# Attention and two feed-forward layers in one kernel: pooled V in one overlapping read, V without zero rows, a split first score, copies moved to VectorE, and a new written order

## The chip, the cores and the metric

The kernel runs on one core of a Trainium2 chip. The core has five engines that take their instructions in order and meet through semaphores: TensorE (PE, with its weight loads PEld), VectorE (DVE), ScalarE (ACT), GpSimd (POOL), and SyncE (SP), which here issues DMAs. The metric is the device time of one execution in microseconds (us). Before the change three runs took 609.0, 609.87 and 610.14 us; the median is 609.87 us.

## The reference, cut to what matters

Two batches of eight heads attend over 768 positions of head size 64. Each query sees the keys nearer than 16 positions, and in the same softmax 24 pooled keys (the maximum over blocks of 32) with pooled values (the mean over blocks of 32). The result, 1536 tokens of 512 features, goes through two feed-forward layers, 512 to 2048 to 512, with different activations.

```
k_sum = k.reshape(B, H, nb, 32, D).max(axis=3)
v_sum = v.reshape(B, H, nb, 32, D).mean(axis=3)
scores_l = where(|pos_q - pos_k| < 16, q @ k.T / sqrt(D), -1e9)
scores_s = q @ k_sum.T / sqrt(D) + log(32)
a = softmax(concat([scores_l, scores_s]))
x = a @ concat([v, v_sum])
r = relu(x @ w_in);  x = (s * r * r + b) @ w_out          # first layer
h = x @ w_in2;       out = max(0.01 * h, h) @ w_out2      # second layer
```

## The kernel before, in words

**Attention in units.** A unit is one of 6 groups of 256 queries with one of 4 pairs of heads, so there are 24 units; units 0 to 7 make the first 512 tokens. Within a unit four windows of 64 queries see 96 near keys each and 24 pooled ones, so a score row has 120 columns. The written codes of a unit's steps are: `s` scores on PE (L207), `x` masked score and its minimum on DVE (L230), `e` exponential on ACT (L246), `r` reciprocal on DVE (L258, L259), `n` normalisation on POOL (L268), `t` transposition on PE (L279), `c` copy out of PSUM on ACT (L287), `o` product with V on PE (L296), `y` and `Y` the high part on ACT (L307) and the low part on DVE (L312) of the result `xt`. The pooled keys are made by `km` on DVE (L121) and put between the near keys by `kp` on POOL (L132, L136). The pooled values come from `p` on PE (L173), `wc` copies them to SBUF (L179), `w` stores them to DRAM in 4 DMAs (L185), and `vs` reads them back to rows 96 to 119 of each V tile, one DMA per window (L195).

**Feed-forward in steps.** Every product is made of three fp32r matmuls (high by high, low by high, high by low). A step is one of 16 slices of 128 hidden features for one chunk of 512 tokens: `I` (L366, two halves of 6 matmuls), `A` and `a` (activation on ACT and on DVE, L377 and L384), `G` and `g` (high part on ACT, L391, low part on DVE, L398), and `O` (L415, four parts of 3 matmuls). There are 96 steps; the first 16 are chunk 0 of the first layer. During these 16 the weights of the first layer come in as 64-bit words of 512 KB per half step: `L` loads one into one of four stage tiles (L320), `R` rescales its upper half on ACT (L326), `B` puts the 32-bit value together on DVE in two instructions (L336, L337) and by that frees the stage tile for a later load. `H` and `lp` or `lv` split a weight tile for use: high part on ACT (L351), low part on POOL (`lp`) or on DVE (`lv`), both at L357.

**What sets the order.** No scheduler moves anything: the string `HEAD` is read from left to right, and each engine, and SP's queue, gets its instructions in that order. The number behind a code is the unit, the half step or the part. From step 33 on a plain loop writes the rest. A wait at the head of one engine's queue therefore holds up all that is written behind it on that engine. All DMAs but three constants and one store are issued by SP.

Of the kernel before, what the change touches and what calls it, by code (L numbers as in the profile page):

```python
# [48 lines left out]
k0 mask q0 iden k1 pool q2 km0 kp0 q1 k2 s0 v1 v0 km1 v2 s1 x0 kp1 L0 e0 k3 s2 x1 q3 e1 s3 r0 vn1 km2 n0 x2 kp2 t0  # L49
e2 r1 s4 x3 n1 q4 c0 r2 s5 x4 e3 n2 t1 t2 q5 c1 x5 e4 r3 n3 c2 r4 p0 n4 e5 t3 p1 c3 r5 p2 n5 R0 km3 t4 wc0 B0 kp3 c4  # L50
t5 w0 s6 c5 H0 L2 s7 x6 lp0 e6 s8 x7 vs0 s9 e7 r6 x8 n6 vs1 x9 t6 e8 r7 n7 o0 vs2 c6 r8 y0 n8 t7 e9 Y0 vn0 o1 vn2 L1
t8 k4 o2 y1 r9 c7 L3 Y1 n9 L4 o3 y2 c8 Y2 t9 y3 o4 c9 Y3 o5 y4 Y4 p3 y5 Y5 o6 R1 o7 R2 B1 y6 o8 y7 Y6 L6 H1 p4 Y7 y8
B2 lp1 R3 I0 wc1 Y8 L8 km4 v3 H2 o9 R4 lp2 B3 I1 y9 B4 kp4 H3 L5 I2 A0 lp3 Y9 L9 H4 s10 a0 v4 lp4 G0 I3 x10 q6 e10
g0 I4 A1 r10 O2 n10 R5 a1 I5 R6 B5 G1 t10 B6 L7 A2 O1 c10 O0 g1 L10 H6 O3 a2 lp6 O5 H5 s11 G2 lp5 R7 g2 I6 R8 x11
e11 O9 B7 I7 B8 R9 L11 O7 R10 r11 O4 L12 A3 B10 n11 O11 H8 O8 a3 H10 L13 lp8 t11 B9 O6 R11 lp10 I8 c11 B11 L14 H7 w1
O10 R12 lp7 I9 G3 B12 L17 R13 g3 L15 I10 H9 k7 B13 R14 lp9 O13 A4 B14 L16 O15 H12 O12 lp12 a4 L23 I11 k5 G4 R15 I12
g4 A5 B15 H14 O17 lp14 a5 O19 L18 R16 O16 km7 R17 I13 B16 kp7 I14 A6 B17 L20 H16 O14 km5 L19 lp16 R18 I15 a6 H11 kp5
B18 G5 O18 s12 H13 g5 L21 G6 I16 lv11 H18 lv13 R19 lp18 O21 g6 R20 O23 B19 A7 O25 R21 O27 B20 L22 q7 O20 x12 O22 L28
# [12 lines left out]
O85 G22 r21 I47 g22 H47 lv47 I48 H50 A23 lp50 t18 a23 I49 c18 G23 o18 A24 g23 H52 t19 n21 a24 I50 y18 c19 Y18 lp52
t20 t21 c20 I51 c21 I52 H54 A25 lp54 o19 a25 I53 y19 Y19 I54 H56 lp56 s22 s23 x22 e22 I55 x23 e23 r22 O91 O90 O95
H58 r23 O94 lp58 O89 O88 O93 G24 O92 H49 g24 o20 H51 lv49 o21 A26 n23 lv51 G25 O99 a26 n22 y21 O97 y20 g25 I56 Y20
A27 Y21 O103 a27 I57 O101 H60 O96 lp60 O98 O100 G26 O102 H53 g26 I58 H55 lp53 A28 t22 G27 a28 lp55 t23 I59 c22 g27
c23 I60 A29 H62 a29 O106 lp62 I61 O107 H64 O105 lp64 O111 O109 O104 O110 H57 O108 G28 lv57 I62 H59 g28 G29 lv59 O115
A30 g29 O112 o22 a30 o23 y22 Y22 O116 y23 Y23 O119 O114 I63 O118 H66 O113 A31 lp66 I64 a31 G30 H61 g30 O117 lv61 I65
H63 G31 lp63 O123 H68 g31 O120 A32 lp68 O121 a32 O122 O125 H65 O126 X5 lv65 O124 G32 Z5 I66 X4 g32 X6 Z4 O127 X7 Z7
O131 Z6 O130 O128 I67 A33 H67 a33 lp67 G33 g33 O129
'''
POOL_BIAS = math.log(BLK)  # L80


@with_exitstack
def block_attention_moe_moe(ctx, tc, q, k, v, vn, w1, w2, mask, ident_in, pool_in, out):
# [13 lines left out]
    soft = pool("soft", 4)  # L98
# [3 lines left out]
    ps_at = pool("ps_at", 2, space=PSUM)  # L102
# [94 lines left out]
    def att_scores(n, ps, tag):  # L197
        g, hp = n
        b, gb = divmod(g, GPB)
        sc = ps.tile([P, 512], F32, name=tag)  # L200
# [13 lines left out]
        scs[n] = sc  # L214

    def att_max(n, ring=None):
# [3 lines left out]
        if ring is None:  # L220
            sm = soft.tile([P, 512], F32, name="sm")[:, : GU * KEYS].rearrange("p (u c) -> p u c", u=GU)
# [6 lines left out]
        for u in range(GU):  # L228
# [10 lines left out]
            )  # L239
        sms[n] = sm, nm  # L240
# [207 lines left out]
    def place(kind, n):  # L448
# [16 lines left out]
        "s": lambda n: att_scores(units[n], *place("s", n)),  # L465
        "x": lambda n: att_max(units[n], wres if n < 8 else None),
# [81 lines left out]
def _layout(q, k, v, moe_w_in, moe_w_out, moe_s, moe_b, moe2_w_in, moe2_w_out):  # L548
# [8 lines left out]
    vp = np.zeros((NG, P, GU, DM), f32)  # L557
    vp[:, :LOC] = vw.reshape(NG, GU, LOC, DM).transpose(0, 2, 1, 3)
# [53 lines left out]
```

## Time and profile before

| what | value |
|---|---|
| median of three runs | 609.87 us |
| span of the profiled execution, first to last instruction | 606.2 us, 3.7 us under that median |
| PE busy | 586.1 us, 97% |
| DVE, ACT, POOL busy | 360.6, 333.1, 196.7 us |
| moved by DMA | 54.33 MB |

The page has no time of the profiled execution other than its span; the 3.7 us stand for what lies around it. Busy times say little on their own here, since the span has two very different parts: the first 126 us or so, in which attention, the conversion of the weights and the first 16 steps share all engines, and the rest, in which PE goes from matmul to matmul.

### The profile page before, as it was taken

How to read it: one execution, taken by the hardware profiler on the slowest of the kernel's cores; microseconds unless marked ns; L12 is line 12 of the kernel's file. 1: busy time of each engine (PE TensorE's matmuls, PEld its weight loads, DVE VectorE, ACT ScalarE, POOL GpSimd, SP SyncE). 2: the span in 40 equal slices, each digit the busy share in tenths (PEclk: the TensorE clock that was granted, in tenths of full speed). 3: DMA queues.
4: the chain of work that ended last, by engine and by line, in shares of the span. 5: the costliest groups of instructions: out<-in, count | busy, mean ns of one | idle time of the engine just before them, and what ended most of it. 6: DMA issues, size and time to landing. Idle time of an engine off the chain costs nothing.

```text
span 606.2 us, 8728 instructions
## 1 busy us (share of the span) xinstructions
PE 586.1 (97%) x3208; PEld 475.0 (78%) x3208; DVE 360.6 (59%) x689; ACT 333.1 (55%) x709; POOL 196.7 (32%) x182
## 2 busy tenths in 40 slices
PE   5799899999999999999999999999999999999997
PEld 4467687777878888888888888888888888888885
DVE  4668997872636334567777867766544444544443
ACT  4978577654648554555555655554544444544442
POOL 2644546354235343223322233222222222222220
PEclk9999999999999999999999999999999999999999
DMA  8897876400024000004342433310100000100001
GB/s 334 288 315 276 271 250 211 165 1 2 1 104 170 2 2 1 0 5 135 104 115 96 139 105 95 118 66 1 70 0 2 0 1 0 71 0 1 0 1 69
DMA packets 17058, 54.33 MB, mean 90 GB/s; under 512 B 2152, under 2 KB 2792, under 8 KB 16376
## 3 DMA queue, kind: packets, MB, share of 16 engines
q1 hardware_dynamic: 16440, 53.29, 26.1%
q10 hardware_dynamic: 576, 0.50, 0.3%
q8 instruction: 25, 0.41, 0.3%
q14 instruction: 17, 0.14, 0.1%
HBM read 50.21 MB, written 3.57 MB: 89 GB/s over the span
## 4 chain that ended last, share of the span: by engine, by line
PE 80%; DVE 9%; DMA 4%; ACT 3%; SPq 1%; issue 1%; POOL 1%; DVEq 0%; POOLq 0%; ACTq 0%
PE h L366 37%; PE acc L417 22%; PE acc L415 18%; DVE w L337 3%; DMA st<-in_w 2%; DVE w L336 2%; DMA kt<-in_k 2%; PE at L207 1%; PE at L296 1%; DVE g L398 1%; ACT st L326 1%; PE at L279 1%; SPq L195 1%; DVE r L384 1%; DVE kp L121 1%
## 5 line engine op out<-in xcount | busy, mean ns | idle before, releaser
L366 PE MATMUL h<-xt,win 128*128 128x512 f32 x1152 | 283.2, 392 | 2.8 <-DVE r L384 2.0
L366 PEld LDWEIGHTS h<-xt,win 128*128 128x128 f32 x1152 | 214.5, 188 | 50.9 <-issue 2.3
L357 POOL TENSOR_TENSOR win<-w,win 128x512 fp32r<-128x512 f32 x96 | 133.3, 1389 | 311.9 <-ACT win L351 308.4
L415 PE MATMUL acc<-g,wout 128*128 128x512 f32 x576 | 144.6, 393 | 1.7 <-DVE g L398 1.7
L417 PE MATMUL acc<-wout,g 128*128 128x512 f32 x576 | 138.2, 389 | 0.0
L415 PEld LDWEIGHTS acc<-g,wout 128*128 128x128 f32 x576 | 106.8, 188 | 25.4 <-DVE g L398 2.5
L417 PEld LDWEIGHTS acc<-wout,g 128*128 128x128 f32 x576 | 108.1, 188 | 22.5
L357 DVE TENSOR_TENSOR wout<-w,wout 128x512 fp32r<-128x512 f32 x78 | 86.6, 1112 | 39.0 <-ACT wout L351 38.8
L379 ACT ACTIVATE r<-h 128x512 f32<-128x512 f32 x48 | 28.7, 597 | 87.5 <-PE h L366 87.5
L386 DVE TENSOR_TENSOR r<-r,h 128x512 f32<-128x512 f32 x48 | 33.0, 688 | 68.6 <-ACT r L379 68.4
L351 ACT CAST wout<-w 128x512 fp32r<-128x512 f32 x96 | 59.5, 620 | 24.1 <-PE acc L415 11.7
L351 ACT CAST win<-w 128x512 fp32r<-128x512 f32 x96 | 59.1, 616 | 19.4 <-PE h L366 15.4
L384 DVE SCALAR_TENSOR_TENSOR r<-r,msk,h 128x512 f32<-128x512 f32 x48 | 35.7, 744 | 33.5 <-ACT r L377 33.2
L337 DVE SCALAR_TENSOR_TENSOR w<-st,w 128x512 int32<-128x512 int32 x64 | 52.4, 819 | 4.8 <-ACT st L326 0.7
L398 DVE SCALAR_TENSOR_TENSOR g<-r,msk,g 128x512 fp32r<-128x512 f32 x48 | 41.2, 858 | 23.7 <-ACT g L391 23.6
L393 ACT CAST g<-r 128x512 fp32r<-128x512 f32 x48 | 29.8, 621 | 36.4 <-DVE r L386 36.4
L391 ACT ACTIVATE g<-r,msk 128x512 fp32r<-128x512 f32 x48 | 34.7, 722 | 23.4 <-DVE r L384 16.1
L326 ACT ACTIVATE st<-st 128x512 f32<-128x512 f32 x64 | 41.7, 673 | 9.9 <-DMA st<-in_w 9.9
L402 DVE TENSOR_TENSOR g<-r,g 128x512 fp32r<-128x512 f32 x48 | 33.1, 690 | 22.6 <-ACT g L393 22.6
L377 ACT ACTIVATE r<-h 128x512 f32<-128x512 f32 x48 | 28.4, 591 | 32.3 <-PE h L366 28.8
L357 POOL TENSOR_TENSOR wout<-w,wout 128x512 fp32r<-128x512 f32 x18 | 25.2, 1401 | 33.9 <-ACT wout L351 33.7
L336 DVE TENSOR_SCALAR w<-st 128x512 int32<-128x512 int32 x64 | 32.4, 506 | 1.7 <-DMA st<-in_w 1.7
(50 smaller groups left out, 307.7 us busy)
## 6 DMA issues: line engine op xcount, KB each, us to landing
st<-in_w SPq DMA_DIRECT2D x64, 512.0 KB
vt<-in_v SPq DMA_DIRECT2D x5, 1024.0 KB
kt<-in_k SPq DMA_DIRECT2D x8, 500.0 KB
out<-kt SPq DMA_DIRECT2D x11, 256.0 KB
q<-in_q SPq DMA_DIRECT2D x8, 256.0 KB
w<-in_vn SPq DMA_DIRECT2D x3, 512.0 KB
w<-in_q SPq DMA_DIRECT2D x4, 256.0 KB
w<-in_v SPq DMA_DIRECT2D x2, 512.0 KB
```

Of the source, the lines that this page charges most:

```text
L326: nc.scalar.activation(out=high, in_=high, func=AF.Prelu, scale=2.0**-112, alpha=2.0**32)
L336: nc.vector.tensor_scalar(f, low, 29, None, op0=ALU.logical_shift_right)
L337: nc.vector.scalar_tensor_tensor(out=f, in0=high, scalar=3, in1=f, op0=ALU.logical_shift_left, op1=ALU.bitwise_or)
L351: nc.scalar.copy(t[:, 0, :], wf[layer, fc][:, half, :])
L357: engine.tensor_sub(t[:, 1, :], wf[layer, fc][:, half, :], t[:, 0, :])
L366: nc.tensor.matmul(hs[i], lhsT=w[:, a, cc * P : (cc + 1) * P], rhs=xt[c][:, b, cc, :], start=(cc == 0 and a == b == 0), stop=(cc == NCC - ...
L384: nc.vector.scalar_tensor_tensor(out=r, in0=r, scalar=sb_sb[:, 0:1], in1=h, op0=ALU.mult, op1=ALU.mult)
L391: nc.scalar.activation(out=gs[i][:, 0, :], in_=rs[i], func=AF.Identity, bias=sb_sb[:, 1:2], scale=1.0)
L398: nc.vector.scalar_tensor_tensor(out=g[:, 1, :], in0=r, scalar=sb_sb[:, 1:2], in1=g[:, 0, :], op0=ALU.add, op1=ALU.subtract)
L402: nc.vector.tensor_sub(g[:, 1, :], r, g[:, 0, :])
L415: nc.tensor.matmul(acc[m], lhsT=w[:, a, ms], rhs=g[:, b, :], start=first, stop=last)
L417: nc.tensor.matmul(acc[m], lhsT=g[:, b, ms], rhs=w[:, a, :], start=first, stop=last)
```

## The change

1. `vs` reads all windows of a tile in one DMA, with an access pattern whose windows overlap in DRAM (24 rows, a stride of 16 rows from window to window): 7 DMAs in place of 24.
2. V lies in DRAM with 96 rows per window in place of 128 of which 32 were zero: 768 KB per group in place of 1024 KB.
3. The three constants (`mask`, `pool`, `iden`) are issued by SP, behind the first keys and queries, not by ACT beside them.
4. The scores of unit 0 are made in two sets of matmuls (`sl`: the 96 near columns, `sp`: the 24 pooled ones).
5. Some copies go from ACT or POOL to DVE: `cv` (for `c`), `yv` (for `y`), `kpv` (for `kp`).
6. The attention tiles `sm` and `at` are named buffers handed out by a small class, so their reuse follows the written order.
7. `HEAD` is written anew; among other things more of the low parts of weights are `lv`, on DVE, and fewer are `lp`.

```
-k0 mask q0 iden k1 pool q2 km0 kp0 q1 k2 s0 v1 v0 km1 v2 s1 x0 kp1 L0 e0 k3 s2 x1 q3 e1 s3 r0 vn1 km2 n0 x2 kp2 t0
+k0 km0 q0 iden kp0 k1 q1 s1 mask km1 x1 e1 pool kp1 sl0 sp0 x0 s3 k2 r1 v0 e0 km2 q2 r0 n1 kp2 s2 x2 t1 e2 x3 r2 cv1
...
+class Slots:
+    def tile(self, key):
+        self.used[key] = i = self.idle.pop(0)
+        return self.pool.tile([P, 512], F32, name=f"{self.name}{i}")
+    def free(self, key):
+        if key in self.used:
+            self.idle.append(self.used.pop(key))
...
-            nc.sync.dma_start(t, v[g][:, us, :])
+            nc.sync.dma_start(t[:LOC], v[g][:, us, :])
...
-            of = vps[b][16 * r0 : 16 * (r0 + n) + 8]
-            for u in range(n):
-                nc.sync.dma_start(t[LOC:KEYS, u, :], of[16 * u : 16 * u + 24])
+            of = vps[b]
+            rows = bass.AP(of.tensor, of.offset + 16 * r0 * DM, [[DM, 24], [16 * DM, n], [1, DM]])
+            nc.sync.dma_start(t[LOC:KEYS], rows)
...
-                    sc[hs, u * KEYS : (u + 1) * KEYS],
+                    sc[hs, u * KEYS : (u + 1) * KEYS].rearrange("p (c j) -> p c j", c=WCH)[:, :, lo:hi],
...
-                    rhs=kt[hs, c0 : c0 + WCH, :],
+                    rhs=kt[hs, c0 : c0 + WCH, lo:hi],
...
-        "mask": lambda: nc.scalar.dma_start(msk_sb, mask),
+        "mask": lambda: nc.sync.dma_start(msk_sb, mask),
...
+        "kpv": lambda x: place_k(x // NHP, x % NHP, nc.vector.tensor_copy),
+        "sl": lambda n: att_scores(units[n], *place("s", n), 0, CH),
+        "sp": lambda n: att_scores(units[n], *place("s", n), CH, CW),
+        "cv": lambda n: att_evac(units[n], nc.vector.tensor_copy),
+        "yv": lambda n: att_hi(units[n], nc.vector.tensor_copy),
...
-    vp = np.zeros((NG, P, GU, DM), f32)
-    vp[:, :LOC] = vw.reshape(NG, GU, LOC, DM).transpose(0, 2, 1, 3)
+    vp = vw.reshape(NG, GU, LOC, DM).transpose(0, 2, 1, 3)
```

What this does to the order shows at three places. The first is SP's queue around the return of the pooled values. `vd` is the DRAM copy of them, `st` a weight half, `in_vn` the V rows of the second batch. Before:

```order
L185 DMA vd<-vparts 26x512 x4
L320 DMA st<-in_w 128x512
L195 DMA vt<-vd 24x512 x8
L195 DMA w<-vd 24x512 x4
L160 DMA w<-in_vn 128x1024 x2
L320 DMA st<-in_w 128x512
L116 DMA kt<-in_k 128x1000
```

and now:

```order
L204 DMA vd<-vparts 26x512 x4
L346 DMA st<-in_w 128x512
L214 DMA vt<-vd 24x4x512 x2
L178 DMA w<-in_vn 128x1024 x3
L346 DMA st<-in_w 128x512
L214 DMA w<-vd 24x2x512 x2
```

Twelve small reads have become four, and all three loads of `in_vn` stand behind the first two of them. The second place is PE's queue at the first steps, where `h` is the result of `I` and `acc` that of `O`. Before:

```order
L366 MATMUL h<-xt_96,win 128x512 x6
L296 MATMUL at<-sm,w 64x64 x8
L366 MATMUL h<-xt_96,win 128x512 x12
L207 MATMUL at<-kt,q_239 64x120 x8
L366 MATMUL h<-xt_96,win 128x512 x12
L415 MATMUL acc<-g,wout 128x512 x3
```

and now:

```order
L320 MATMUL at_612<-sm_597,w 64x64 x8
L301 MATMUL at_630<-ident,sm_574 120x128 x4
L392 MATMUL h<-xt_96,win 128x512 x48
L320 MATMUL at_733<-sm_713,w 64x64 x8
L441 MATMUL acc<-g,wout 128x512 x24
```

The first `O` stood behind 30 matmuls of `I` and two attention steps; it stands behind 48 and one now, and steps 1 and 0 change places. The third place is DVE's queue at the same point, up to the low part `g` that the first `O` reads (`win` is a split weight, `kp` pooled keys, `r` an activation). Before, from the last of the low parts of `xt` for chunk 0 on:

```order
L312 TENSOR_TENSOR xt_96<-h,xt_96 128x256 x2
L336 TENSOR_SCALAR w<-st 128x512
L337 SCALAR_TENSOR_TENSOR w<-st,w 128x512
L312 TENSOR_TENSOR xt_97<-at,xt_97 128x256
L121 TENSOR_REDUCE kp<-kt 128x24
L336 TENSOR_SCALAR w<-st 128x512
L337 SCALAR_TENSOR_TENSOR w<-st,w 128x512
```

and now, from the second `km` after the same point to that `g`:

```order
L139 TENSOR_REDUCE kp<-kt 128x24
L410 SCALAR_TENSOR_TENSOR r<-r,msk,h 128x512
L362 TENSOR_SCALAR w<-st 128x512
L363 SCALAR_TENSOR_TENSOR w<-st,w 128x512
L410 SCALAR_TENSOR_TENSOR r<-r,msk,h 128x512
L383 TENSOR_TENSOR win<-w,win 128x512
L424 SCALAR_TENSOR_TENSOR g<-r,msk,g 128x512
L310 COPY sm_713<-at_630 120x512
L139 TENSOR_REDUCE kp<-kt 128x24
L362 TENSOR_SCALAR w<-st 128x512
L363 SCALAR_TENSOR_TENSOR w<-st,w 128x512
L424 SCALAR_TENSOR_TENSOR g<-r,msk,g 128x512
```

Two activations, a low part of a weight, a copy out of PSUM and a conversion now stand ahead of the `g` that the first `O` needs.

## Rows read from the trace of the kernel before

**Rows 1.** Stretches: length, busy time of PE, PEld, DVE, ACT, POOL, clock, DMA

```profile
0.00:39.24 39.24, 27.53 (x385) 20.04 (x385) 20.66 (x116) 27.76 (x105) 15.91 (x33) 1.00 0.86 313
...
60.00:90.00 30.00, 27.73 (x134) 22.05 (x134) 27.99 (x46) 18.69 (x33) 14.81 (x14) 1.00 0.76 256
...
120.00:150.00 30.00, 28.84 (x166) 22.85 (x166) 15.07 (x25) 15.76 (x30) 14.82 (x13) 1.00 0.01 3
150.00:606.20 456.20, 452.29 (x2191) 371.96 (x2189) 254.20 (x404) 233.88 (x446) 126.83 (x100) 1.00 0.15 49
```

**Rows 2.** Chain that ended last, first 70 us and a late matmul run: start, us, what

```profile
0.74 4.65 DMA kt<-in_k
...
6.98 3.49 PE acc L207 x32
...
19.14 1.62 ACT w L246 x8
...
21.82 0.54 ACT vparts L179
...
23.58 1.93 DMA vd<-vparts
...
31.29 5.86 DMA st<-in_w
...
596.87 5.47 PE acc L417 x24
```

**Rows 3.** Timeline of PE: start, us, line, count [idle before, its releaser]

```profile
39.24 1.66 PE L366 MATMUL h<-xt,win 128*128 128x512 f32 x6
...
74.40 1.61 PE L366 MATMUL h<-xt,win 128*128 128x512 f32 x6 [0.83 <-DVE r L384]
...
104.51 0.60 PE L279 MATMUL at<-ident,sm 128*120 128x128 f32 x4
...
112.53 1.04 PE L207 MATMUL at<-kt,q 64*64 64x120 f32 x16
...
125.59 1.66 PE L366 MATMUL h<-xt,win 128*128 128x512 f32 x6 [0.92 <-DVE r L384]
```

**Rows 4.** Stretches again: ACT's in the fill, and DVE's up to two of its instructions

```profile
9.22:39.02 29.80, 25.22 (x366) 17.79 (x362) 18.20 (x111) 26.26 (x104) 14.73 (x27) 1.00 0.88 324
...
39.52:103.28 63.76, 60.68 (x350) 47.45 (x350) 57.15 (x114) 44.71 (x101) 33.92 (x33) 1.00 0.78 267
39.52:125.54 86.02, 81.63 (x490) 63.15 (x489) 75.50 (x156) 59.64 (x139) 43.43 (x42) 1.00 0.67 228
```

**Rows 5.** Timeline of SP: start and us of issuing, the DMA, count

```profile
25.59 3.14 SPq L195 DMA_DIRECT2D vt<-vd  x8
```

**Rows 6.** Groups of DVE from 60 to 90 us: busy us, mean ns

```profile
L337 DVE SCALAR_TENSOR_TENSOR w<-st,w 128x512 int32<-128x512 int32 x13 | 11.5, 883 | 1.3
L336 DVE TENSOR_SCALAR w<-st 128x512 int32<-128x512 int32 x12 | 8.0, 666 | 0.0
...
L384 DVE SCALAR_TENSOR_TENSOR r<-r,msk,h 128x512 f32<-128x512 f32 x4 | 3.0, 739 | 0.0
...
L357 DVE TENSOR_TENSOR wout<-w,wout 128x512 fp32r<-128x512 f32 x2 | 1.3, 686 | 0.0
```

**Rows 7.** Groups of DVE from 320 to 600 us

```profile
L337 DVE SCALAR_TENSOR_TENSOR w<-st,w 128x512 int32<-128x512 int32 x21 | 14.5, 693 | 0.9
L336 DVE TENSOR_SCALAR w<-st 128x512 int32<-128x512 int32 x21 | 8.8, 419 | 0.0
```

**Rows 8.** Groups over the whole span: POOL's weight split, copies on DVE and ACT

```profile
L357 POOL TENSOR_TENSOR win<-w,win 128x512 fp32r<-128x512 f32 x96 | 133.3, 1389 | 311.9 <-ACT win L351 308.4 <-DVE rec L259 2.0 <-issue 1.3
...
L287 ACT COPY w<-at 120x512 f32<-120x512 f32 x8 | 4.6, 572 | 0.4 <-PE at L279 0.4
...
L438 DVE COPY kt<-acc 128x512 f32<-128x512 f32 x6 | 3.9, 685 | 1.3 <-PE acc L417 1.3
```

**Rows 9.** Timeline of ACT: a rescaling that waited for its weights

```profile
69.46 0.68 ACT L326 ACTIVATE st<-st 128x512 f32<-128x512 f32 x1 [1.94 <-DMA st<-in_w]
```

More of the change, by code (lines that the diff above doesn't have):

```diff
@@ L54 @@
[L54 to L58, printed above, removed]
@@ new lines @@
+O27 y11 B15 R26 Y10 G7 q8 Y11 I21 L28 t13 c13 H15 s14 H17 L29 B26 H26 s15 x15 I18 G8 x14 I19 lp15 H22 g7 L31 O29 A10
+lv22 g8 lp17 O30 O28 e14 B19 o13 yv13 A9 r14 Y13 o12 a9 R27 G9 O31 O34 B27 n14 L25 R24 O35 lp26 e15 I22 t14 O33 r15
+c14 R21 I23 O32 n15 y12 I26 g9 R30 a10 t15 Y12 H19 G10 q9 cv15 lp19 I27 g10 A11 B24 O39 O36 H23 H24 a11 O37 O38 A13
+B21 o14 H21 G11 lp24 o15 y15 I24 B30 yv14 a13 Y14 lp21 Y15 I25 R29 s17 A12 s16 H30 R31 g11 x17 v4 O41 lv30 R28 lp23
+O42 B31 O40 O44 vs5 O46 O43 B28 H28 a12 I30 G12 R25 H27 O45 B25 lv28 G13 O47 H25 g12 H34 lv27 I31 I28 lv25 B29 O49 x16
@@ L79, with __init__ @@
+O105 O109 O111 a28 O104 G28 O108 G29 cv23 H60 g29 H59 I62 lv60 o22 o23 g28 H57 lv57 I63 A31 I60 a31 O115 H64 I61 lp64
+O113 O114 y23 lp59 A30 yv22 Y23 O112 O118 a30 G30 H61 O116 O119 g30 O117 lv61 G31 O120 O122 H66 O121 O123 Y22 I64 lv66
+I65 H63 lp63 g31 A32 O125 H65 lp65 O126 O127 X5 a32 X6 X7 I66 G32 Z6 I67 H68 A33 O124 g32 Z5 O129 Z7 lv68 O131 X4 H67
+Z4 O128 a33 G33 g33 lp67 O130
 '''
 POOL_BIAS = math.log(BLK)
+class Slots:
+    def __init__(self, pool, name, n):
+        self.pool, self.name, self.idle, self.used = pool, name, list(range(n)), {}
+    def tile(self, key):
[4 more added lines that the diff above has]
+            self.idle.append(self.used.pop(key))
@@ L101, in block_attention_moe_moe, with psum @@
     ps_h = pool("ps_h", 2, space=PSUM)
-    ps_at = pool("ps_at", 2, space=PSUM)
+    ps_at = Slots(pool("ps_at", space=PSUM), "at", 2)
+    def psum(ring, tag, key):
+        return ring.tile(key) if tag == "at" else ring.tile([P, 512], F32, name=tag)
     ident = const.tile([P, P], F32, name="ident")
@@ L127, in max_k, with place_k @@
         kps[b, hp] = kp
-    def place_k(b, hp):
+    def place_k(b, hp, copy=nc.gpsimd.tensor_copy):
         t = kts[b, hp]
         src = kps.pop((b, hp)).rearrange("p (j g) -> p g j", g=WCH)
-        nc.gpsimd.tensor_copy(
+        copy(
             t[:, 0:48, CH:CW].rearrange("p (a g) j -> p a g j", g=WCH),
@@ L135, in place_k @@
         )
-        nc.gpsimd.tensor_copy(t[:, 48:50, CH:CW], src[:, 0:2, :])
+        copy(t[:, 48:50, CH:CW], src[:, 0:2, :])
     def load_q(pair, hp):
@@ L164, in pool_v @@
         if part == 0:
-            vac[b] = ps_at.tile([P, 512], F32, name="at")
+            vac[b] = ps_at.tile(("v", b))
         for j in range(PC):
@@ L192, in load_vs, with att_scores @@
             r0 = (gb * GU + us.start) % 3
-            of = vps[b][16 * r0 : 16 * (r0 + n) + 8]
-            for u in range(n):
-                nc.sync.dma_start(t[LOC:KEYS, u, :], of[16 * u : 16 * u + 24])
-    def att_scores(n, ps, tag):
+            of = vps[b]
+            rows = bass.AP(of.tensor, of.offset + 16 * r0 * DM, [[DM, 24], [16 * DM, n], [1, DM]])
+            nc.sync.dma_start(t[LOC:KEYS], rows)
+    def att_scores(n, ps, tag, lo=0, hi=CW):
         g, hp = n
         b, gb = divmod(g, GPB)
-        sc = ps.tile([P, 512], F32, name=tag)
+        if lo == 0:
+            scs[n] = psum(ps, tag, ("s", n))
+        sc = scs[n]
         qt = qts[g // 2, hp].rearrange("p w (x e) -> p w e x", e=2)
@@ L220, in att_max @@
         if ring is None:
-            sm = soft.tile([P, 512], F32, name="sm")[:, : GU * KEYS].rearrange("p (u c) -> p u c", u=GU)
+            sm = soft.tile(("m", n))[:, : GU * KEYS].rearrange("p (u c) -> p u c", u=GU)
         else:
@@ L239, in att_max @@
             )
+        ps_at.free(("s", n))
         sms[n] = sm, nm
@@ L263, in att_norm @@
         if n not in sns:
-            sns[n] = soft.tile([P, 512], F32, name="sm")
+            sns[n] = soft.tile(("n", n))
         sn = sns[n][:, : GU * KEYS].rearrange("p (u c) -> p u c", u=GU)
@@ L273, in att_norm @@
             )
+        soft.free(("m", n))
     def att_transpose(n, ps, tag):
-        tp = ps.tile([P, 512], F32, name=tag)
+        tp = psum(ps, tag, ("t", n))
         sn = sns.pop(n)
@@ L279, in att_transpose, with att_evac @@
             nc.tensor.transpose(tp[:KEYS, u * P : (u + 1) * P], sn[:, u * KEYS : (u + 1) * KEYS], ident)
+        soft.free(("n", n))
         tps[n] = tp
-    def att_evac(n):
+    def att_evac(n, copy=nc.scalar.copy):
         tp = tps.pop(n)
@@ L285, in att_evac @@
         if at is None:
-            at = soft.tile([P, 512], F32, name="sm")[:KEYS, :].rearrange("p (u c) -> p u c", u=GU)
-        nc.scalar.copy(at.rearrange("p u c -> p (u c)"), tp[:KEYS, :])
+            at = soft.tile(("a", n))[:KEYS, :].rearrange("p (u c) -> p u c", u=GU)
+        copy(at.rearrange("p u c -> p (u c)"), tp[:KEYS, :])
         ats[n] = at
+        ps_at.free(("t", n))
     def att_out(n, ps, tag):
         g, hp = n
-        av = ps.tile([P, 512], F32, name=tag)
+        av = psum(ps, tag, ("o", n))
         vt, at = vts[g], ats.pop(n)
@@ L303, in att_out, with att_hi @@
         avs[n] = av
-    def att_hi(n):
+        soft.free(("a", n))
+    def att_hi(n, copy=nc.scalar.copy):
         g, hp = n
-        nc.scalar.copy(xt[g // 2][:, 0, hp, (g % 2) * GT : (g % 2 + 1) * GT], avs[n][:, :GT])
+        copy(xt[g // 2][:, 0, hp, (g % 2) * GT : (g % 2 + 1) * GT], avs[n][:, :GT])
     def att_lo(n):
```

53 lines of the change are left out of this document (25 added, 28 removed).

## The prediction

> **What bounds the kernel now.** I read the stretches first [rows 1]. After 150 us TensorE (PE) is busy 452.3 of 456.2 us, and the 3.9 us left over are the tail behind the last matmul: there it goes from matmul to matmul, 24 in 5.47 us or 0.228 us each [rows 2], and a new order can give nothing. What can be won lies before: PE stands idle 11.7 us of the first 39.2, 2.3 us from 60 to 90 and 1.2 us from 120 to 150 [rows 1]. The granted clock is 1.00, the upper level, in all of these rows.
>
> Then the chain of waits and PE's timeline, for who holds it up. The first 39 us are the fill, the attention for 512 tokens; the first matmul of a feed-forward step starts at 39.24 us [rows 3]. The chain there goes from the first keys (4.65 us of DMA) to the first scores at 6.98, through ScalarE (ACT) with exponentials of 1.62 us a unit, to the copy of the pooled values at 21.82, SP's DMAs of them, and a weight half that needs 5.86 us from 31.29 on [rows 2]. ACT is busy 26.3 of 29.8 us between its first exponential and the last high part [rows 4]. After the fill VectorE (DVE) is the bound: 28.0 of 30 us busy from 60 to 90 [rows 1]. PE's two long waits, 0.83 us at 74.40 and 0.92 us at 125.59, both ended with DVE's activation at L384 [rows 3].
>
> **The change, part by part.** *First keys and constants.* The 500 KB of first keys no longer share the DMA engines with constants; about 0.2 MB of these moved beside them. At 313 GB/s [rows 1] that is up to 0.6 us; I take 0.4, so scores start near 6.5 and the first exponential near 8.8 instead of 9.22. The bounds are 0 and 0.6. In the new order the first score read by ACT is of unit 1 and needs its pooled keys, so the split of unit 0 (`sl`, `sp`) starts nothing earlier: it adds 8 short matmuls, 0 to 0.9 us by a whole unit of 0.97 us (112.53 to 113.50, less the overlap, [rows 3]); I take 0.35.
>
> *Fill on ACT.* Up to the last high part of chunk 0 ACT had 10 exponentials, 10 copies `c`, 1 `wc`, 3 `R`, 1 `H`, 8 `y`. It now has 10, 5, 2, 4, 3 and 6. Five copies of 0.57 us [rows 8] and two shorter `y` leave; one `wc`, one `R` (0.68 [rows 9]) and two `H`, of about that length, come: 1.1 us less, 25.2 us of busy time. Before, 3.5 of the 29.8 us were waits [rows 4]; I take 4.4, since two new waits show in DVE's order (`x2` behind `r0`, `x4` behind `r2`, each of which waits for ACT). From 8.8 us on that ends at 38.4, and DVE's last low part of chunk 0 comes at 39.2, against 39.5 before. The gain is what DVE has done by then: four conversions `B` and one weight split in place of two `B`. PE gets its first feed-forward step near 37.4, since that step's first half needs only units 0 to 3.
>
> *Pooled values.* Eight of the 12 reads took SP 3.14 us to issue [rows 5], so 12 take 4.7 and four take 1.6: 3.1 us go. The loads of `in_vn` and the late weight half, whose landing let ACT go on at 37.17 before, move up by this and by about 1.5 us that `wc` is earlier. It is hidden: what is late next is ACT's own queue, counted above. It is worth 0 here and 1.2 us if ACT were done sooner.
>
> *V without zero rows.* 0.77 MB less lie ahead of the first pooling, 2.5 us of DMA at the fill's 313 GB/s [rows 1]. Pooling then waits for the buffer that the first `cv` frees, not for V: that copy stands behind a reciprocal of the third exponential, 8.8 + 3 x 1.62 us [rows 2] + about 2 us of waits = 15.7, and ends near 16.4. So nothing is counted; the bounds are 0 and the 2.5 us. [...] No row of this trace shows a transfer of 96 rows. [...]
>
> *Copies and splits on DVE.* I count DVE from the last low part of chunk 0 to the low part of unit 10, which in both orders stands just ahead of the same transposition of unit 13 on PE (104.51 us [rows 3]). Before: 39.52 to 103.28, 63.8 us, 57.2 busy [rows 4]. The new order has 4 `B` fewer (0.42 + 0.69 us undisturbed [rows 7]), 2 `a` and 2 `g` fewer (0.74 [rows 6]), and 2 `cv` (0.69 [rows 8]), 3 `lv` (0.69 [rows 6]) and 2 `kpv` more. No row shows `kpv` on DVE; 200 elements in two copies lie between 0.2 and 1.0 us, and I take 0.5. Sum: -4.4 - 3.0 + 1.4 + 2.1 + 1.0 = -2.9 us. Then GpSimd (POOL): from 60 to 90 the two instructions of `B` took 883 and 666 ns against 693 and 419 later on [rows 6, 7], 13 x 0.19 + 12 x 0.25 = 5.4 us beside 14.8 us of POOL [rows 1], or 0.37 us per us. POOL has 7 `lp` of 1.39 us [rows 8] and one `kp` less, 10.7 us. At 0.3, since DVE isn't always busy, -3.2 us; the bounds are 0 and -4.0. So that low part comes at 39.2 + 63.8 - 6.1 = 96.9. PE by then has done 27 matmuls fewer than before (two `I`, five `O`), 6.2 us: 96.9 + 6.2 = 103.1 against 104.5, a lead of 1.4 us.
>
> On the way the first `O` waits: PE can end eight `I` and one `o` near 49.3, but `g` of step 0 stands behind a conversion whose weight half is asked for only after the sixth `B`, and comes near 51.5. That costs 2 us of idle PE, inside the sum above, as the lead there is 2.3 us (three `I` more done than at 49.7 before).
>
> *What the old order lost afterwards.* From 104.51 to 125.59 PE did 63 feed-forward matmuls (14.4 us) and two each of `s`, `t`, `o`, about 3.7 us, in 21.1 us: about 2.5 us, bounds 2 and 3, were lost, the wait for `a` of step 12 among them. In the new order DVE reaches that `a` about 3 us later than 125.5, but PE has 9.7 us more behind it (two `I`, six `O`, one `s`, one `t`, two `o`), so this wait is gone. The lead is 1.4 + 2.5 = 3.9 us. From step 33 on both orders are one loop.
>
> I take off 0.5 us for waits of the new order that I can't see. The profiled execution would go from a span of 606.2 to 602.8 us; with the 3.7 us that lie around it, that is 606.5 against the median of 609.87.
>
> **The rivals.** *DVE waits for weights (slower).* A stage tile is loaded again only when a `B` frees it; ACT waited up to 1.94 us for one [rows 9]. The new order takes conversions of later steps (halves 14, 18) early and puts loads of queries and keys that wait for PE between weight loads on SP. If DVE stands 1 us longer at each of eight such `B` before unit 10's low part, that comes at 104.9, the lead of 1.4 turns into -6.6, and with 2.5 us regained later and the 0.5 taken off the end is near 614.5. Against it: DVE was idle only 2 us of 30 with the same four tiles [rows 1]. It makes the kernel slower from about 4.6 us of such waits on.
>
> *POOL's relief fails (no change).* If DVE's instructions stay as long as before although POOL does less, 3.2 us are missing: the lead at the transposition is -1.8, at the end 0.7 less 0.5, near 609.7. For it: it is an average over unlike stretches. Against it: the same instruction has both lengths in one trace.
>
> *Larger gain.* If ACT waits 1 us in the fill, not 4.4, DVE's queue and all behind it come that much earlier: 606.5 - 3.4 = 603.1. For it: half the copies have left ACT's queue. Against it: the two waits named above, and the 3.5 us before.
>
> **How the numbers follow.** My forecast has a chance of 0.45, the larger gain 0.18, no change 0.2, slower 0.17. The runs tell nothing below 0.2% (1.2 us) from no change. Faster is the forecast, the larger gain: 0.63; same 0.2; slower 0.17. The range goes from the larger gain, with 0.5 us more for the bounds of keys and relief, 602.5, to 611, short of the slow case; about 0.12 is left out there and 0.07 below. The forecast alone reaches from 604.8 to 608.3.
>
> **What would show it.** Right: first feed-forward matmul at 37 to 38 us, unit 10's low part on DVE near 97, a PE gap of about 2 us ahead of the first `O` near 50, no wait for step 12's `a`, and the same matmul rate from 150 us on. Wrong: DVE gaps ended by weight DMAs between 45 and 95 us (slower), `B` still near 1.5 us where POOL is idle, or a first `O` before 49.

## The result, and the profile after

The changed kernel takes 617.32 us (median of five runs, 612.6 to 617.7) against 610.14 us for the kernel before beside it (609.0 to 610.45): a ratio of 1.0102, 95% interval [1.008, 1.0124]. It is slower by 1%; I had forecast 606.5 us and a range up to 611.

The stretches of the changed kernel, columns as in [rows 1] (length, busy time of PE, PEld, DVE, ACT, POOL, granted clock, DMA share, GB/s; the last row is from 10 to 20 us):

```profile
0.00:39.24 39.24, 25.91 (x294) 19.81 (x295) 20.34 (x113) 20.46 (x83) 14.20 (x31) 0.87 0.93 271
60.00:90.00 30.00, 26.71 (x161) 21.66 (x160) 22.06 (x69) 17.29 (x47) 8.31 (x8) 0.94 0.84 258
...
150.00:615.50 465.50, 460.46 (x2195) 379.35 (x2194) 265.16 (x408) 231.59 (x435) 123.14 (x98) 1.00 0.14 44
10.00:20.00 10.00, 6.51 (x66) 4.64 (x64) 6.25 (x45) 7.12 (x37) 5.08 (x10) 0.83 1.01 236
```

The same 10 us of the kernel before:

```profile
10.00:20.00 10.00, 7.96 (x98) 5.83 (x98) 6.61 (x51) 9.37 (x45) 5.89 (x11) 1.00 1.01 414
```

Read the last two rows against each other. The DMA engines are busy all the time in both, and in the changed kernel they move 236 GB/s in place of 414. That is when V is loaded, in 96 rows, with some loads of queries, keys and weights beside it. The clock column is the mean granted clock of TensorE as a share of its upper level; 0.83 says that PE ran at the lower one, 0.50, for part of the time: the mean is 0.51 from 15.3 to 18.7 us. After 150 us nothing is new: PE is busy 460.5 of 465.5 us, against 452.3 of 456.2 before [rows 1].

The chain that ended last in the changed kernel, its first 33 us (start, us, what):

```profile
2.58 5.18 DMA w<-in_q
7.79 13.29 DMA w<-in_v
...
21.12 1.92 PE at L191 x10
...
23.06 0.59 ACT vparts L197
...
24.86 2.60 DMA vd<-vparts
...
27.96 5.18 DMA vt<-vd
...
33.18 1.12 PE h L320 x16
```

In [rows 2] the fill went through the exponentials of ACT. Now it goes through DMAs: 13.29 us from the issue of the last V load to its landing (10.15 in the run with V in 128 rows below), then the pooling, and 5.18 us for reading pooled values back.

PE's timeline at the places that the prediction names, and at some of its waits (start, us, line, count, in brackets the idle time ahead and what ended it); it answers to [rows 3]:

```profile
14.87 1.48 PE L228 MATMUL acc<-kt,w 64*64 64x120 f32 x16 [2.14 <-DMA w<-in_q]
...
29.49 0.62 PE L301 MATMUL at<-ident,w 128*120 128x128 f32 x4 [1.54 <-DVE rec L279]
...
31.95 0.78 PE L320 MATMUL h<-w,vt 120*64 120x64 f32 x16 [1.84 <-DMA vt<-vd]
...
33.18 1.12 PE L320 MATMUL h<-w,vt 120*64 120x64 f32 x16 [0.45 <-DMA vt<-vd]
...
45.04 1.17 PE L392 MATMUL h<-xt,win 128*128 128x512 f32 x4
...
58.27 0.73 PE L441 MATMUL acc<-g,wout 128*128 128x512 f32 x2 [0.92 <-ACT g L417]
...
76.78 2.47 PE L228 MATMUL at<-kt,q 64*64 64x120 f32 x22 [2.33 <-DMA q<-in_q]
...
107.02 0.62 PE L301 MATMUL at<-ident,sm 128*120 128x128 f32 x4
...
110.36 1.39 PE L228 MATMUL at<-kt,q 64*64 64x120 f32 x16 [1.74 <-ACT sm L310]
...
144.67 2.66 PE L392 MATMUL h<-xt,win 128*128 128x512 f32 x11
```

The first feed-forward step starts at 45.04 us, not at 37.4 as I said or at 39.24 as before. Waits for queries, at 14.87 and 76.78, and for a copy of ACT at 110.36 are new. The gap ahead of the first `O`, forecast as about 2 us near 50, is 0.92 us at 58.27. The row at 144.67 runs on through the first half of step 14 and shows no wait for DVE's activation, where [rows 3] had 0.92 us.

### The profile page after: what moved, and what is told of

Same layout as the page of the kernel before. It is cut to its first block, busy times and chain, and to the rows that moved or that the text cites. A ratio compares the mean times of both kernels' runs of the same rounds, so it can differ in the third digit from the quotient of the medians.

```text
span 615.5 us, 8722 instructions
## 1 busy us (share of the span) xinstructions
PE 590.7 (96%) x3224; PEld 481.6 (78%) x3224; DVE 371.7 (60%) x728; ACT 321.4 (52%) x687; POOL 175.4 (29%) x165
## 4 chain that ended last, share of the span: by engine, by line
PE 82%; DMA 10%; DVE 4%; ACT 2%; issue 1%; SPq 1%; ACTq 0%; DVEq 0%
PE h L392 38%; PE acc L443 21%; PE acc L441 18%; DMA st<-in_w 5%; PE at L228 2%; DMA w<-in_v 2%; DMA q<-in_q 1%; PE at L320 1%; PE at L301 1%; DVE w L363 1%; DMA w<-in_q 1%; DMA vt<-vd 1%; DVE g L424 1%; PE h L320 1%; DVE w L362 1%; PE at L191 1%
## 5 line engine op out<-in xcount | busy, mean ns | idle before, releaser
L383 POOL TENSOR_TENSOR win<-w,win 128x512 fp32r<-128x512 f32 x78 | 109.1, 1399 | 298.7 <-ACT win L377 283.1
L383 DVE TENSOR_TENSOR wout<-w,wout 128x512 fp32r<-128x512 f32 x73 | 82.6, 1133 | 36.3 <-ACT wout L377 36.2
L410 DVE SCALAR_TENSOR_TENSOR r<-r,msk,h 128x512 f32<-128x512 f32 x48 | 35.6, 744 | 28.6 <-ACT r L403 28.1
L363 DVE SCALAR_TENSOR_TENSOR w<-st,w 128x512 int32<-128x512 int32 x64 | 45.5, 711 | 5.6 <-ACT st L352 2.4
L383 POOL TENSOR_TENSOR wout<-w,wout 128x512 fp32r<-128x512 f32 x23 | 31.1, 1358 | 57.5 <-ACT wout L377 52.2
L289 POOL TENSOR_TENSOR sm<-sm,rec 128x384 f32<-128x384 f32 (+1 forms) x32 | 22.0, 708 | 46.1 <-DVE rec L280 35.8
```

What stands on the lines that cost most here:

```text
L363: nc.vector.scalar_tensor_tensor(out=f, in0=high, scalar=3, in1=f, op0=ALU.logical_shift_left, op1=ALU.bitwise_or)
L383: engine.tensor_sub(t[:, 1, :], wf[layer, fc][:, half, :], t[:, 0, :])
L410: nc.vector.scalar_tensor_tensor(out=r, in0=r, scalar=sb_sb[:, 0:1], in1=h, op0=ALU.mult, op1=ALU.mult)
```

## Experiments: V in 96 rows

**V in 128 rows again, all else as changed.**

```diff
-            nc.sync.dma_start(t[:LOC], v[g][:, us, :])
+            nc.sync.dma_start(t, v[g][:, us, :])
-    vp = vw.reshape(NG, GU, LOC, DM).transpose(0, 2, 1, 3)
+    vp = np.zeros((NG, P, GU, DM), f32)
+    vp[:, :LOC] = vw.reshape(NG, GU, LOC, DM).transpose(0, 2, 1, 3)
```

> The changed kernel with V loaded in 128 rows again (the last 32 of them zeros), all else as changed. Theory A: the 96-row transfers slow every DMA of the fill (8192-byte packets of 455 to 561 ns, 230 GB/s at 10 to 20 us, against 309 ns and about 427 GB/s before); then the packets take about 309 ns again, the first feed-forward matmul comes near 39 to 40 us instead of 45.0, and the time is 608 to 612 us. Rival B: the written order of the fill (loads of queries behind V on SP, DVE's order) costs the 5.8 us; then the first feed-forward matmul stays near 44 to 45 us and the time near 617 us.

Measured: 610.12 us (12 runs), ratio to before 0.9999 [0.9984, 1.0015]. Theory A holds for the time: the ratio falls by 1.03%, 6.3 us. It holds for the packets too (the pieces in which the trace records a DMA): all but a few of the 8192-byte ones from 10 to 20 us took 309 ns, where half of those in the changed kernel took 515 to 573. Its first step came at 42.43 us, neither the 39 to 40 of A nor the 44 to 45 of B, so part of the late fill is something else. From 10 to 20 us, and the first attention output and the first step on PE:

```profile
10.00:20.00 10.00, 7.89 (x88) 4.15 (x84) 7.58 (x53) 8.86 (x46) 6.21 (x12) 1.00 1.01 408
...
29.61 1.12 PE L320 MATMUL h<-w,vt 120*64 120x64 f32 x16 [2.20 <-DMA vt<-vd]
...
42.43 0.94 PE L392 MATMUL h<-xt,win 128*128 128x512 f32 x3
```

**The kernel before, with only V in 96 rows** (the same edit the other way round).

> The kernel before with V loaded in 96 rows and nothing else changed. Theory A: its packets slow to 450 to 560 ns, the first feed-forward matmul comes 1 to 4 us after 39.24 us, and the time is 611 to 615 us. Rival B: no slower than before, 608 to 610 us, since 0.77 MB less are read.

Measured: 614.67 us, ratio 1.0075 [1.0049, 1.0102]: theory A again, with an order that nobody touched. From 10 to 20 us it moves 248 GB/s, and its first feed-forward step came at 42.51 us against 39.24 [rows 3]. The clock was 1.00 up to 60 us in this profile, so here the fill was late without it.

```profile
10.00:20.00 10.00, 7.60 (x88) 5.21 (x84) 6.61 (x51) 9.37 (x44) 6.03 (x12) 1.00 1.02 248
```

**The 96 rows in two transfers**, `t[:64]` and `t[64:LOC]`, in the changed kernel.

> The changed kernel with the 96 rows of V loaded by two transfers, of 64 and of 32 rows. If it is how one transfer of 96 rows is dealt to the DMA engines that makes its packets slow, they take 300 to 400 ns and the time is 609 to 613 us. [...]

Measured: 619.12 us, ratio 1.0152 [1.0122, 1.0182], slower than the 609 to 613 us expected, and 232 GB/s from 10 to 20 us (half of the 8192-byte packets there took 519 to 626 ns). Cutting one transfer in two doesn't help.

```profile
10.00:20.00 10.00, 7.20 (x75) 4.62 (x74) 7.33 (x51) 7.75 (x40) 5.07 (x10) 0.83 1.00 232
```

**112 rows**, in the run with 128.

```diff
-            nc.sync.dma_start(t, v[g][:, us, :])
+            nc.sync.dma_start(t[:112], v[g][:, us, :])
```

> As the run with V in 128 rows, with V loaded in 112 rows (the last 16 of them zeros). If any transfer short of 128 rows slows the DMA engines as 96 rows do, its packets take 450 ns or more and the time is 614 to 618 us. [...]

Measured: 617.92 us, ratio 1.0139 [1.0104, 1.0174], and 289 GB/s. Half of the 8192-byte packets from 10 to 20 us took 380 to 444 ns, less than the 450 expected; the time, within the 614 to 618 us expected, says that 112 rows are no better than 96.

```profile
10.00:20.00 10.00, 6.90 (x70) 4.62 (x70) 7.04 (x49) 7.90 (x41) 5.07 (x10) 0.83 1.02 289
```

So the loss goes with how V is loaded, in either written order: while it came in 64 + 32, 96 or 112 rows the engines moved 232 to 289 GB/s, and 408 to 414 with 128. Other loads under way are slowed with it: the median packet of the queries (2048 bytes) from 10 to 20 us took 141 ns in the changed kernel and 84 in the run with 128 rows, that of the keys (4000 bytes) 275 and 155. In all of these edits the rows and the place of a group in DRAM change together (768 or 896 KB from group to group, not 1024); no run changes one alone.

## Experiments: the written order

With V in 128 rows the changed kernel only equals the one before, and 3.4 us of the forecast are still missing. Some of PE's waits in that run up to 130 us (us in total, times, longest):

```profile
...
PE h L320 <- DMA vt<-vd: 2.4, 2, 2.2
PE at L301 <- DVE rec L279: 1.7, 1, 1.7
...
PE at L228 <- ACT sm L310: 1.4, 1, 1.4
PE at L228 <- DMA q<-in_q: 1.2, 1, 1.2
```

**Loads of queries earlier.**

```diff
- k2 r1 v0 e0 km2 q2 r0
+ k2 r1 q2 v0 e0 km2 r0
- G2 v5 H10 L11 q6 O5 H5 O3 R9 q7
+ G2 q6 q7 v5 H10 L11 O5 H5 O3 R9
```

> As the run with V in 128 rows, and three loads of queries moved ahead of V loads on SP (the third of the fill ahead of the first V load, two later ones ahead of the V load that they stood behind). If these queues cost what the trace of the changed kernel shows (PE waits of 2.1 us at 14.9 and of 2.3 us at 76.8 for queries), it is 2 to 4 us faster than the run without this edit, 605 to 609 us; if DVE or ACT is late in any case, it is the same within 1 us.

Measured: 609.0 us, ratio 0.9988 [0.9968, 1.0008], the same as without. PE no longer waited for queries, and other waits stood in their place: 1.72 us for V at 19.53, and 1.92 us at 77.67 for a weight split on ACT, where a rescaling just ahead had waited 2.75 us for its weights.

**Pooled values ahead of a weight half on SP.**

```diff
- w0 L2 r5 vs0 vs1 c3
+ w0 r5 vs0 vs1 L2 c3
```

> As the run with V in 128 rows, with the two overlapping reads of pooled values for the first 512 tokens ahead of a weight half (L2) on SP instead of behind it. There PE waited 2.2 us at 29.6 us for the first of these reads, 5.1 us after its issue. If the 0.5 MB of weights ahead of it in the queues make it late, that wait falls below 1 us, the first feed-forward matmul comes 1 to 2 us before 42.4 us, and the time is 0.5 to 2 us below 610. If one read of 24 rows is slow by itself, the wait stays above 1.5 us and the time within 0.5 us.

Measured: 609.36 us, ratio 0.9993 [0.9976, 1.001]; the time can't be told from 610. The trace shows the mechanism: the wait fell from 2.20 us to 0.34 and the first attention output came at 27.62 instead of 29.61.

```profile
27.62 1.12 PE L320 MATMUL h<-w,vt 120*64 120x64 f32 x16 [0.34 <-DMA vt<-vd]
```

So it was the 0.5 MB in the queue ahead that made the read late. The first feed-forward step came at 40.73 us instead of 42.43, as the first theory said, and next to nothing of these 1.7 us is left in the time.

**The copy of unit 4 ahead of two score passes on DVE.**

```diff
- n5 x6 x7 vn0 s8 vn2 e6 cv4 t5
+ n5 cv4 x6 x7 vn0 s8 vn2 e6 t5
```

> As the run with V in 128 rows, with the copy of the transposed unit 4 (on VectorE in the changed kernel) ahead of the score passes of units 6 and 7 on VectorE instead of behind them. There PE stood 1.7 us at 26.8 us, for the buffer that this copy frees. If moving copies to VectorE brought a new wait into the fill, that gap goes and the time falls by 0.5 to 1.5 us; if PE is held by the pooled values right behind it in any case, the gap moves to the first attention output and the time is the same within 0.5 us.

Measured: 609.86 us, ratio 1.0009 [0.9994, 1.0025]. The gap ahead of `t5` went, and moved to the attention output behind it, as the second theory said (2.20 us before, 3.58 now):

```profile
25.13 0.65 PE L301 MATMUL at<-ident,w 128*120 128x128 f32 x4
29.35 0.89 PE L320 MATMUL h<-w,vt 120*64 120x64 f32 x12 [3.58 <-DMA vt<-vd]
```

**One late load of V moved back** (`v5`, from beside `H10` to behind `L28`).

> As the run with V in 128 rows, with the 1 MB load of V for tokens 1280 to 1535 (first used beyond 130 us) issued near 107 us instead of 67 us. It stands ahead of a weight half (L11), two loads of queries and a load of keys there, and PE waits 1.2 us at 74.3 us for queries and 1.4 us at 106.5 us. If the order of loads on SP costs time from 60 to 90 us, the DMA share there falls from 0.84 to 0.75 or less, these waits shrink and the time falls by 1 to 3 us; if ScalarE and VectorE are late by themselves, it is the same within 0.5 us.

Measured: 608.27 us, ratio 0.9978 [0.9964, 0.9992]: faster than the kernel before, and 0.21% below the run without this edit, at the edge of what the two intervals tell. The DMA share from 60 to 90 us falls from 0.84 to 0.79, less than I said, but PE's wait for queries goes and PE is busy 28.75 of 30 us instead of 26.94.

```profile
60.00:90.00 30.00, 28.75 (x177) 23.22 (x176) 25.51 (x73) 21.71 (x60) 11.81 (x11) 1.00 0.79 272
```

**All of these together** (of the loads of queries only `q6` and `q7`).

> V in 128 rows with all three changes of order (pooled values ahead of the weight half, the copy of unit 4 earlier, the late V load later), and two loads of queries ahead of the weight half they stood behind. If these waits are what ate the gain that was forecast for the new order, it is 604 to 607.5 us, faster than the kernel before; if each wait only gives way to the next, 608.5 to 610.5 us.

Measured: 607.03 us, ratio 0.9964 [0.9948, 0.9981]: faster than both kernels, and clear of the run with V in 128 rows alone. So part of the missing gain was in these waits, 2.1 us of the 3.4. PE is busy all of the 30 us from 60 to 90.

```profile
0.00:39.24 39.24, 29.60 (x350) 21.90 (x351) 23.59 (x121) 23.93 (x95) 15.03 (x33) 0.91 0.89 311
60.00:90.00 30.00, 30.00 (x183) 24.54 (x183) 25.18 (x73) 21.91 (x60) 13.10 (x12) 1.00 0.79 264
```

**The one wide read of pooled values, alone in the kernel before.**

> The kernel before with one overlapping read of pooled values for a buffer (24 rows of 4 windows) in place of one read for a window, nothing else changed. My prediction: SP has issued the first 12 reads 3.1 us earlier, hidden behind ScalarE: the time is 608.5 to 610 us. Rival: the wide read is slower to land (5.1 us from issue in the changed kernel's chain), the first attention output starts later than 28.7 us, and the time is 610 to 612 us.

Measured: 610.1 us, ratio 1.0004 [0.999, 1.0018]. SP issues the first four reads in 1.5 us, where 8 of the old 12 took 3.14 [rows 5]. It gives nothing, though, and the rival's sign is there: the first attention output came at 29.48 us, behind a wait of 0.35 for this read, where it started at 28.72 in the kernel before, without one. First the kernel before, then this run:

```profile
28.72 1.18 PE L296 MATMUL h<-w,vt 120*64 120x64 f32 x16
```

```profile
29.48 0.69 PE L296 MATMUL h<-w,vt 120*64 120x64 f32 x16 [0.35 <-DMA vt<-vd]
```

## Experiments: the clock

Even with all changes of order the clock is 0.91 up to 39.24 us (above). The trace puts the lower level from 28.6 to 35.4 us, behind a PE wait of 2.26 us ahead of the first attention output, and from 55.9 to 59.3 us, behind one of 1.34 us ahead of the first `O`. For these three runs PE got matmuls on the identity to do in its waits; they write a bank that the real product then overwrites.

```diff
         av = psum(ps, tag, ("o", n))
+        for _ in range({(0, 0): 14, (1, 0): 6}.get(n, 0)):
+            nc.tensor.matmul(av[:, :P], lhsT=ident, rhs=ident, start=True, stop=True)
...
             acc[m] = ps_acc.tile([P, 512], F32, name="acc")
+            for _ in range(9 if i == 0 and m == 2 else 0):
+                nc.tensor.matmul(acc[m][:, :P], lhsT=ident, rhs=ident, start=True, stop=True)
```

> As the run with all changes of order, with matmuls on the identity (their results are overwritten) put where PE waits: 14 of about 0.125 us ahead of the first attention output, 6 ahead of the second, 9 ahead of the first matmul into the output accumulators. There the granted clock is at its lower level from 28.6 to 35.5 and from 55.9 to 59.3 us, behind PE waits of 2.3 and 1.3 us, and the same matmuls take up to twice as long. If idle PE is what lowers the clock, both stretches go back to the upper level and the time falls by 2 to 3 us, to 604 to 605.5 us. If the clock falls for another reason, the stretches stay and the time is 607 to 608 us.

Measured: 606.84 us, ratio 0.9959 [0.9945, 0.9974]. The clock was 1.00 throughout (it had been 0.91 up to 39.24 us and 0.92 from there to 60), so idle PE is what lowers it here; but the time is that of the run without, so what the lower clock costs stays open. Each of these matmuls took about 0.25 us, twice what I had counted. The first 14 did not outlast their wait: PE stood 0.62 us more for the read, which came later in this profile, as the last V load did. Behind the other two groups no wait was left, so they may have held up real work; that is not shown.

**Half as many (7, 3 and 5).**

> As the run with filled gaps, with about half as many matmuls on the identity (7, 3 and 5): there each took 0.245 us and not 0.125, so that 14, 6 and 9 of them outlasted the waits that they filled, and the time did not move although the granted clock was at the upper level throughout. If the lower clock costs time, the shorter filling gives 1 to 2.5 us against the run with all changes of order (607.0), 604.5 to 606 us. If what PE loses at the lower clock is waited for elsewhere anyway, the time stays at 606.5 to 607.5 us.

Measured: 606.22 us, ratio 0.9948 [0.9929, 0.9968], the fastest of all and faster than both kernels. Against the run without filling the intervals overlap, so a gain of 0.8 us is not shown in the time. In the fill the two profiles show one: the first attention output starts 0.4 us later than without filling (28.04 against 27.65), and the first feed-forward step 1.7 us earlier (39.44 against 41.14). First this run, then the one without:

```profile
28.04 0.69 PE L322 MATMUL h<-w,vt 120*64 120x64 f32 x16 [0.34 <-DMA vt<-vd]
...
30.55 1.04 PE L228 MATMUL at<-kt,q 64*64 64x120 f32 x16
31.52 1.15 PE L322 MATMUL h<-w,vt 120*64 120x64 f32 x32
...
39.44 1.86 PE L394 MATMUL h<-xt,win 128*128 128x512 f32 x7
```

```profile
27.65 0.69 PE L320 MATMUL h<-w,vt 120*64 120x64 f32 x16 [2.26 <-DMA vt<-vd]
...
30.21 1.87 PE L228 MATMUL at<-kt,q 64*64 64x120 f32 x16
32.00 1.97 PE L320 MATMUL h<-w,vt 120*64 120x64 f32 x32
...
41.14 1.17 PE L392 MATMUL h<-xt,win 128*128 128x512 f32 x4
```

The same 16 matmuls of a score take 1.04 us in the one and 1.87 in the other.

The length of one wait doesn't decide here whether the clock falls. The run with one wide read in the kernel before has the lower level from 30.2 to 37.0 us (0.91 up to 39.24) behind waits of 1.35, 0.35 and 0.56 us, and the run with V in 128 rows keeps the upper one (1.00 from 39.24 to 60 us) behind a wait of 1.45 us at 56.19. Nor is the kernel before free of it, though [rows 1] shows none: of its 94 executions beside these runs 15 had a mean granted clock of 0.994 or less, which was one such stretch of 6.8 us in the profile just named. Their median is 610.28 us, against 609.69 for the 56 at 0.999 or more.

**The changed kernel itself with filled waits** (8 ahead of unit 4's scores, 7 ahead of the first attention output, 9 and 6 ahead of the scores of units 11 and 15).

> The changed kernel itself (V in 96 rows), with matmuls on the identity where PE waits ahead of its stretches at the lower clock: 8 ahead of the scores of unit 4 (wait of 2.1 us at 14.9), 7 ahead of the first attention output (1.8 us at 32), 9 ahead of the scores of unit 11 (2.3 us at 76.8), 6 ahead of those of unit 15 (1.7 us at 110.4). If the lower clock (17 us in all) makes a good part of the loss, the time falls by 2 to 5 us from 617.3, to 612.5 to 615.5 us. If the waits alone make it, it stays at 616.5 to 618 us.

Measured: 612.77 us, ratio 1.0061 [1.0041, 1.0081], against 1.0102 without: 0.41%, 2.5 us by the ratios and 4.5 by the medians. By the two intervals the gain is 0.7 to 4.3 us. Every transfer and order is the same, and the clock up to 39.24 us is 1.00 in place of 0.87 with the DMA rate as low as ever (273 GB/s, against 271); the first step comes at 42.29 us instead of 45.04:

```profile
0.00:39.24 39.24, 28.94 (x374) 22.20 (x378) 22.65 (x119) 23.19 (x94) 14.28 (x32) 1.00 0.93 273
```

So about 2.5 us of the changed kernel's time are matmuls at a clock of 0.50 behind waits of about 2 us. How much of that belongs to the 6.3 us that the rows of V cost is not shown: with V in 128 rows PE has 6.8 us at the lower level too (29.5 to 36.3; 0.91 up to 39.24), and the filling mends the like of it here.

## Why the prediction was wrong

The profiled executions, cut at the first feed-forward step (us; the last column is the span less the first):

| kernel | first step | span | first step to end |
|---|---|---|---|
| before | 39.24 | 606.2 | 567.0 |
| my forecast | 37.4 | 602.8 | 565.4 |
| changed | 45.04 | 615.5 | 570.5 |
| changed, V in 128 rows | 42.43 | 610.0 | 567.6 |
| and all changes of order | 41.14 | 606.2 | 565.1 |
| and half filling | 39.44 | 604.1 | 564.7 |

One execution can lie 2 to 3 us from its kernel's median, so small differences here count for little. The fill is where most went wrong, 7.6 of 12.7 us. In the medians the miss is 10.8 us; by the ratios it is 9.6, of which 6.3 are the rows of V; the rest is the forecast gain, which was not there with V in 128 rows either.

- **The step that failed: "V without zero rows", "So nothing is counted; the bounds are 0 and the 2.5 us."** The lower bound excluded a loss with no reason from a row: I had written that no row shows a transfer of 96 rows, and still took fewer bytes to be no slower; while they came in the engines moved 236 GB/s, against 408 with 128 rows. It costs 6.3 us in the changed kernel and 4.6 in the one before. Nor does pooling wait "for the buffer that the first `cv` frees, not for V": its last part waited for V, which landed at 21.08 us, and at 18.56 even in 128 rows.
- **A term that was missing: the clock.** It was 1.00 in all rows of before, and I took PE's time for the same matmuls to be fixed. Behind waits of 1.5 to 2.3 us it fell to 0.50 for 17 us in all (15.3 to 18.7, 32.4 to 39.2, 76.8 to 80.2, 110.9 to 114.3); filling these waits gave back about 2.5 us.
- **"Pooled values ... hidden".** This step failed too, and it is what the runs show of the missing gain. I counted SP's time to issue the reads and nothing for their landing. As in the kernel before, a 0.5 MB weight half stands between storing and reading these, and PE waited for the wide read: 1.84 us at 31.95, and 2.20 us at 29.61 with V in 128 rows, 5.1 us after its issue at 24.50, against 3.2 us with that weight half behind it. Mended alone it gave no time, with the other changes of order 2.1 us; where the rest of the gain went stays open. ACT's queue, which I had as the next to be late, was not: it stood 4.6 us waiting for attention outputs. The first exponential starts at 8.71 us (I said 8.8), but by luck: scores start at 5.45 us and not near 6.5, and then DVE's first pass waits for the second keys and, up to 8.39, for `mask`.
- **"Copies and splits on DVE": right for the work, not for the waits.** From its last low part of chunk 0 to that of unit 10 DVE took 59.6 us with 48.8 busy (I had 57.7, from 39.2 to 96.9, and 51.1, 57.2 less 6.1). So it stood 10.8 us in place of 6.6, 5.9 of them for ACT and 1.5 for weights. POOL's relief is there: from 60 to 90 us, with POOL busy 8.31 us in place of 14.81 [rows 1], the two instructions of `B` took 695 and 574 ns, against 883 and 666 [rows 6] and 693 and 419 from 320 to 600 us [rows 7]. `kpv` took 0.34 + 0.17 us the first time and 1.26 + 0.15 the second; I had 0.5, an estimate that no row showed.

```profile
L363 DVE SCALAR_TENSOR_TENSOR w<-st,w 128x512 int32<-128x512 int32 x10 | 7.0, 695 | 1.1 <-ACT st L352 0.6
L362 DVE TENSOR_SCALAR w<-st 128x512 int32<-128x512 int32 x9 | 5.2, 574 | 0.6 <-DMA st<-in_w 0.5
```

- **"The old order lost afterwards" 2.5 us: half right.** The wait for `a` of step 12 is gone. In its place PE waited 1.74 us at 110.36 for a copy on ACT, and ACT had stood 2.91 us for weights just ahead of it, as in my slower rival, on ACT more than on DVE:

```profile
108.56 0.67 ACT L352 ACTIVATE st<-st 128x512 f32<-128x512 f32 x1 [2.91 <-DMA st<-in_w]
109.13 0.71 ACT L417 ACTIVATE g<-r,msk 128x512 fp32r<-128x512 f32 x1
109.74 0.57 ACT L310 COPY sm<-at 120x512 f32<-120x512 f32 x1
```

- **That rival, "DVE waits for weights"**, had the right sign and named the loads that wait on SP, but the size was wrong: DVE itself stood 1.5 us for weights in this stretch, in two waits and not in eight of 1 us. With V in 128 rows such waits and those of the fill ate a part of what DVE had won: four changes of place in the order gave 0.35% back (ratios 0.9999 and 0.9964).
- The 3.7 us "around" the span were not there: in the changed kernel's profiled run it is 1.8 (617.32 less 615.5), and 2.0 in executions of the kernel before (609.32 less 607.3). The profile of before had thus caught an execution of about 608.2 us, 1.7 under its median. In the forecast the two cancel, so they are no part of the miss.

Open: even with the filling, the first step comes 2.0 us later than I said. The pooled values are still read at 28.04 us there, so the fill is set by V, the pooling and the way through DRAM, not by ACT; a kernel that shortens this way was not tried. Nor do the runs tell why fewer than 128 rows are slow. The constants on SP, the split score, the copies on DVE and the named buffers were not run one by one, so what each of them gives or costs is not shown.

## What to carry to other kernels

Fewer bytes need not be a faster load when the load has fewer rows (here 236 GB/s from 10 to 20 us with V in 96 rows, 408 in 128, at a DMA share of 1.01 in both): if the trace shows no transfer of that shape, the bounds must hold a loss, and one run of the old kernel with only that edit settles it. When a stretch of DMAs bounds the start, compare GB/s at a DMA share of 1, not the share. And count a wait of PE twice where the clock may fall behind it (here to 0.50, for 3.4 us and more at a time): once for the wait, once for the matmuls behind it.

## What was unexpected of the hardware

- While V was loaded in 64 + 32, 96 and 112 rows the DMA engines moved 232, 236 to 248 and 289 GB/s, busy throughout, and with 128 rows 408 to 414. The median packet of 8192 bytes took 558 ns with 96 rows in the changed kernel and 309 with 128, and packets of other loads under way grew too: 141 ns against 84 for 2048 bytes, 275 against 155 for 4000.
- PE's granted clock fell from 1.00 to 0.50 behind PE waits of 1.7 to 2.3 us near 15, 32, 77 and 110 us in the changed kernel, and was 1.00 from 0 to 120 us when matmuls on the identity filled these waits, with the same loads. A score of 16 matmuls took 1.87 us at 0.50 (30.21 us, with all changes of order) and 1.04 at 1.00 (30.55 us, with half filling).
